# Attention and gated FFN in one kernel: the high parts of the gate and value weights cast on VectorE, and the filler products of the identity tied one behind each stage of a unit

## The chip, the cores and the metric

The kernel runs on one core of one Trainium2 chip. The metric is device time in microseconds (us). Three runs of the kernel before took 1180.95, 1181.29 and 1181.86 us, so the median is 1181.29 us.

A core has these engines: PE (TensorE, matrix products; PEld are its weight loads), DVE (VectorE), ACT (ScalarE), POOL (GpSimd) and SP (SyncE), which here only issues DMAs. Each engine works through its own queue in order. An instruction that needs another engine's result waits on a semaphore, and everything behind it in its queue waits too.

## The reference, cut to what matters

```python
# q_l, k_l, v_l: 8 batches, 8 heads, 512 tokens, 64 dims;  q_g, k_g, v_g: 32 global tokens
# w_gate, w_val: 512 x 1536 float64;  w_out: 1536 x 512 float64
s_l  = concat([q_l @ k_g.T, where(|i - j| <= 32, q_l @ k_l.T, -1e9)]) / 8
out_l = softmax(s_l) @ concat([v_g, v_l])              # local tokens
out_g = softmax(q_g @ concat([k_g, k_l]).T / 8) @ concat([v_g, v_l])
x    = concat([out_g, out_l]) -> (8 * 544 tokens, 8 heads * 64)
y    = (sigmoid(x @ w_gate) * (x @ w_val)) @ w_out
```

The result is needed close to float32. The FFN multiplies with a one-pass format (F32R), so each of its operands is split into a high part and a low part, and three products (high by high, low by high, high by low) are summed. The three weights arrive as float64 and are turned to float32 on the chip.

## The kernel before, in words

The tokens are cut into chunks: chunk 0 is blocks 0 and 1 (of 128 tokens each) of batch 0, chunk 1 is blocks 2 and 3 of batch 0 and its global tokens, and chunks 2 to 8 are batches 1 to 7. Chunk 9 is the FFN of all global tokens. For each chunk the attention of 8 heads is computed and then its FFN in 12 steps f of 128 hidden columns (`ffn_stream`, L384).

**Attention of a unit** (`local_unit`, L224) is two blocks of one head, in four stages: scores on PE (L234); mask and row minimum on DVE (L248) and the exponential on ACT (L251); the sums' reciprocals and the scaling into `p_buf` on DVE (L254, L255, L218); four transposes on PE (L270), copied out by ACT (L278); the products with the values on PE (L293, L294), copied out by ACT (L297). A pair of heads is then split into high and low by ACT and POOL (`x_split`, L370 to L373). Chunk 0 has eight units, one for each head, and nothing to overlap with but each other, since the first FFN product (L400) needs its attention.

**Weights** (`convert`, L128) come in 36 pieces of 128x512, three for each f (gate, value, out). Each one is loaded by SP into one of three buffers (L126), ACT takes the exponent's offset out of the upper words (L137), DVE shifts the lower words and joins the two (L139, L140) into one of two buffers, ACT casts the joined words to F32R, which is the high part (L141), and POOL subtracts it from the joined words, which leaves the low part (L142). Gate and value pieces stay in SBUF (`wg`, `wv`); out pieces go to DRAM and are read back at each FFN step.

**Fillers** (`fill`, L108) are products of the 128x128 identity with itself into a PSUM bank that nobody reads. `FILL = (8, 1)`: eight at the beginning, and one behind each PE stage of a unit of chunk 0 (`T["first"]`; L236, L272, L296), 32 in all. Each appears as two PE records (this holds for every product in plain float32; a transpose is one record).

**What sets the order.** The kernel writes its instructions down in an order that a list of events with due times gives: chunk 0's attention is all due before the FFN stream begins, the conversion of f is due at -2 + 4 f FFN units, and attention of the following chunks lies between FFN steps. The program that is run comes from a scheduler that puts the instructions of each engine in a queue order by when it thinks that they can start, and among those that can, takes what was written first. A filler has no input but the identity, so nothing ties it to the place where it was written. `tc.issue_after(ins)` ties what a block issues behind `ins` on the same engine's queue; it adds no semaphore.

Of the kernel before, what the change touches and what calls it, by code (L numbers as in the profile page):

```python
# [17 lines left out]
P = 128  # L18
# [10 lines left out]
VS = (2, 3, 6, 7)  # L29
# [13 lines left out]

HOLE = (8, 1)

FILL = (8, 1)
START = dict(per0=4, base1=1, per1=1.1, base2=23, per2=3, x2=28, lead=8, native_heads=4)
CONVERT = (-2, 4, 1, 3)
CONVERT_EARLY = (-985, -980, -977)
# [10 lines left out]
def kernel(ctx, tc, qk, v, w_gate, w_val, w_out, out_l, out_g):  # L60
    nc = tc.nc
# [15 lines left out]
    ident = const.tile([P, P], F32, name="ident")  # L77
# [27 lines left out]

    fill_ps = ps.tile([P, DM], F32, name="bank_o3")

    def fill(n):  # L108
        for i in range(n):
            nc.tensor.matmul(fill_ps[:, 0:P], ident, ident, start=True, stop=True)  # L110

    fill(FILL[0])
    conv_bufs = []
    anchor, exp_at = [None], [None]

# [6 lines left out]
    def stage(i):  # L122
        if i < len(w_src):
            src = w_src[i]
            st = conv_bufs[0][i % len(conv_bufs[0])].rearrange("p (t n) -> p t n", t=src.shape[1])
            nc.sync.dma_start(st, src)  # L126

    def convert(i, hi, lo):  # L128

        src = w_src[i]  # L130
        t, n = src.shape[1], src.shape[2] // 2
        st, v = (o[i % len(o)].rearrange("p (t n) -> p t n", t=t) for o in conv_bufs)
        words = st.rearrange("p t (n two) -> p t n two", two=2)
        low, high = words[:, :, :, 0], words[:, :, :, 1]
        vf, hf = v.bitcast(F32), high.bitcast(F32)
        with tc.issue_after(exp_at[0].ins) if i < 3 else nullcontext():
            nc.scalar.activation(hf, hf, AF.Prelu, scale=2.0 ** -112, alpha=-2.0 ** 32)  # L137
        with tc.issue_after(anchor[0].ins) if i < 3 else nullcontext():
            nc.vector.tensor_scalar(v, low, 29, None, op0=ALU.logical_shift_right)  # L139
            nc.vector.scalar_tensor_tensor(v, high, 3, v, op0=ALU.logical_shift_left, op1=ALU.bitwise_or)  # L140
        nc.scalar.copy(hi, vf)  # L141
        nc.gpsimd.tensor_tensor(lo, vf, hi.bitcast(F32), op=ALU.subtract)  # L142
        stage(i + len(conv_bufs[0]))

    def convert_w(f, i):
        fs = slice(f * P, (f + 1) * P)
        w = (wg, wv)[i]
        convert(3 * f + i, w[0][:, :, fs], w[1][:, :, fs])

    def convert_wo(f):  # L150
        hi, lo = (spl.tile([P, 1, DM], F32R, name=nm, tag="kl") for nm in ("wo_hi", "wo_lo"))
        convert(3 * f + 2, hi, lo)
        nc.sync.dma_start(wo_dram[f][:, 0], hi[:, 0].bitcast(F32))
        nc.sync.dma_start(wo_dram[f][:, 1], lo[:, 0].bitcast(F32))


    def qcol(j):
        return j * P if j < 2 else Q1 + (j - 2) * P
# [55 lines left out]
    def scaled(kind, out, in_, by):  # L214
        if NORM[kind][cnt["norm"] % len(NORM[kind])] == "s":
            nc.scalar.mul(out, in_, by)
        else:
            nc.vector.tensor_scalar(out, in_, by, None, op0=ALU.mult)  # L218
        cnt["norm"] += 1

    def span(j):
        return (32 if j == 0 else 0), (WIN - 32 if j == 3 else WIN)

    def local_unit(T, blocks, x32s, h, b0):  # L224
        ks, k0s, q0 = T["qk"], T["k0"], T["q0"]
        nat = T["native"]
        last = len(ks) - 1
        s_ps = ps.tile([P, 2, 256], F32, name="bank_x", tag="att", bufs=4)
        for i, j in enumerate(blocks):
            qj = ks[0][:, qcol(j) - q0:qcol(j) - q0 + P]  # L230
            w0, w1 = span(j)
            for t, (kt, k0) in enumerate(zip(ks, k0s)):
                js = slice(k0 + j * BLK + w0, k0 + j * BLK + w1)
                nc.tensor.matmul(s_ps[:, i, w0:w1], qj, kt[:, js], start=t == 0, stop=t == last)  # L234
        if T["first"]:
            fill(FILL[1])  # L236
        if T["first"]:
            s_sb = ffn.tile([P, 2, WIN], F32, name="s_first", tag="ob", bufs=2)
        else:
            s_sb = att.tile([P, 2, WIN], F32, name="s_sb", bufs=1)  # L240
        nm = small.tile([P, 2], F32, name="nm")
        sm = small.tile([P, 2], F32, name="sm")
        r = small.tile([P, 2], F32, name="r")
        pb = p_bufs[cnt["p"] % 2 if T["first"] else 0]
        cnt["p"] += 1
        for i, j in enumerate(blocks):
            w = slice(*span(j))
            anchor[0] = nc.vector.tensor_tensor_reduce(  # L248
                out=s_sb[:, i, w], in0=s_ps[:, i, w], in1=mid[:, w], scale=-0.125, scalar=3.0e38,
                op0=ALU.add, op1=ALU.min, accum_out=nm[:, i:i + 1])  # L250
            exp_at[0] = nc.scalar.activation(s_sb[:, i, w], s_sb[:, i, w], AF.Exp, bias=nm[:, i:i + 1], scale=-1.0,  # L251
                                             accum_out=sm[:, i:i + 1])
        yield
        nc.vector.tensor_scalar_add(r, sm, 1e-9)  # L254
        nc.vector.reciprocal(r, r)  # L255
        flat = pb.rearrange("p a c -> p (a c)")
        joint = blocks[0] == 0 and blocks[1] == 3
        for i, j in enumerate(blocks):
            main = s_sb[:, i, 32:224].rearrange("p (a c) -> p a c", c=96)[:, :, 0:64]
            m0, s0 = 256 * i, (0 if joint else 256 * i) + P + (64 if j == 3 else 0)  # L260
            scaled(nat, flat[:, m0:m0 + P].rearrange("p (a c) -> p a c", c=64), main, r[:, i:i + 1])
            n = 2 if j in (0, 3) else 3
            side = s_sb[:, i].rearrange("p (a c) -> p a c", c=32)[:, 3 * (j == 0):7:3][:, 0:n]
            scaled(nat, flat[:, s0:s0 + 32 * n].rearrange("p (a c) -> p a c", c=32), side, r[:, i:i + 1])
        yield
        nt = 3 if joint else 4
        side_at = (1, 1) if joint else (1, 3)
        pt_ps = ps.tile([P, 4, P], F32, name="bank_y", tag="att", bufs=4)[:, 0:nt]
        for t in range(nt):
            nc.tensor.transpose(pt_ps[:, t], flat[:, t * P:(t + 1) * P], ident)  # L270
        if T["first"]:
            fill(FILL[1])  # L272
        if nat:
            if T["first"] and h % 2:
                pt = ffn.tile([P, 4, P], F32, name="pt_first", tag="th", bufs=1)[:, 0:nt]
            else:
                pt = att.tile([P, 4, P], F32, name="pt_nat", tag="pt", bufs=1)[:, 0:nt]
            nc.scalar.copy(pt, pt_ps)  # L278
        else:
            pt = att.tile([P, 2, 4, P], F32R, name="pt", bufs=1)[:, :, 0:nt]  # L280
            nc.scalar.copy(pt[:, 0], pt_ps)
            nc.vector.tensor_tensor(pt[:, 1], pt_ps, pt[:, 0].bitcast(F32), op=ALU.subtract)  # L282
        yield
        vt = T["v"]
        if h // 2 not in x32s:
            x32s[h // 2] = att.tile([P, 512], F32, name="x32")
        prow = 64 * (h % 2)
        b1, step = blocks[0] - b0, blocks[1] - blocks[0]
        dst = x32s[h // 2][prow:prow + 64].rearrange("p (i c) -> p i c", c=P)[:, b1:b1 + step + 1:step]
        if nat:  # L290
            o_ps = ps.tile([64, 2, P], F32, name="bank_x", tag="att", bufs=4)
            for i, j in enumerate(blocks):
                nc.tensor.matmul(o_ps[:, i], vt[:, VM[j], :], pt[:, 2 * i], start=True, stop=False)  # L293
                nc.tensor.matmul(o_ps[:, i], vt[:, VS[j], :], pt[:, side_at[i]], start=False, stop=True)  # L294
            if T["first"]:
                fill(FILL[1])  # L296
            nc.scalar.copy(dst, o_ps)  # L297
            return
        o_ps = ps.tile([P, 2, 2, P], F32, name="bank_x", tag="att", bufs=4)
        for i, j in enumerate(blocks):  # L300
            nc.tensor.matmul(o_ps[:, i], vt[:, VM[j], :], pt[:, :, 2 * i, :], start=True, stop=False)  # L301
            nc.tensor.matmul(o_ps[:, i], vt[:, VS[j], :], pt[:, :, side_at[i], :], start=False, stop=True)  # L302
        t0 = att.tile([64, 2, 2, P], F32, name="t0", tag="t0", bufs=1)
        nc.scalar.copy(t0, o_ps[64:128])  # L304
        nc.vector.tensor_tensor(t0, o_ps[0:64], t0, op=ALU.add)  # L305
        nc.gpsimd.tensor_tensor(dst, t0[:, :, 0], t0[:, :, 1], op=ALU.add)  # L306
# [217 lines left out]
    for ci in range(3, G):  # L524
        at, width = HOLE
# [7 lines left out]
    for f in range(NF):  # L533
        at = a0 + f * step
# [83 lines left out]
```

## Time and profile before

The profiled execution took 1179.81 us; its span, from the first instruction to the last, is 1177.9 us, so 1.9 us lie around the span.

| engine | busy us | share of the span | instructions |
|---|---|---|---|
| PE | 1146.4 | 97% | 6596 |
| PEld | 962.3 | 82% | 6596 |
| DVE | 773.7 | 66% | 2132 |
| ACT | 753.2 | 64% | 1737 |
| POOL | 413.3 | 35% | 408 |

A share is a mean over stages with different limits. The beginning (attention of chunk 0 alone), the stretch in which the weights are converted, and the rest have to be read apart. A busy PE is not always useful: the fillers count as busy.

### The profile page before, as it was taken

How to read it: one execution, taken by the hardware profiler on the slowest of the kernel's cores; microseconds unless marked ns; L12 is line 12 of the kernel's file. 1: busy time of each engine (PE TensorE's matmuls, PEld its weight loads, DVE VectorE, ACT ScalarE, POOL GpSimd, SP SyncE). 2: the span in 40 equal slices, each digit the busy share in tenths (PEclk: the TensorE clock that was granted, in tenths of full speed). 3: DMA queues.
4: the chain of work that ended last, by engine and by line, in shares of the span. 5: the costliest groups of instructions: out<-in, count | busy, mean ns of one | idle time of the engine just before them, and what ended most of it. 6: DMA issues, size and time to landing. Idle time of an engine off the chain costs nothing.

```text
span 1177.9 us, 19115 instructions
## 1 busy us (share of the span) xinstructions
PE 1146.4 (97%) x6596; PEld 962.3 (82%) x6596; DVE 773.7 (66%) x2132; ACT 753.2 (64%) x1737; POOL 413.3 (35%) x408
## 2 busy tenths in 40 slices
PE   8999999999999999999999999999999999999998
PEld 7777788888888888888888888888888888888897
DVE  5677657577676677667676677667676677533343
ACT  5898877566675676666675676666675675532343
POOL 2444435334353444334352444334452443100000
PEclk9999999999999999999999999999999999999999
DMA  8888844333443343343343343343344342122143
GB/s 295 283 288 279 259 134 128 95 116 94 115 116 113 106 115 98 106 140 90 113 115 114 105 116 98 107 149 91 103 116 122 99 118 81 44 100 72 54 151 118
DMA packets 59489, 151.81 MB, mean 129 GB/s; under 512 B 6144, under 2 KB 19456, under 8 KB 59392
## 3 DMA queue, kind: packets, MB, share of 16 engines
q1 hardware_dynamic: 59392, 150.59, 42.2%
q8 instruction: 52, 0.85, 0.3%
q14 instruction: 45, 0.37, 0.1%
HBM read 135.36 MB, written 15.20 MB: 128 GB/s over the span
## 4 chain that ended last, share of the span: by engine, by line
PE 75%; DVE 11%; ACT 8%; issue 3%; DMA 2%; POOL 1%; SPq 0%; ACTq 0%; DVEq 0%; POOLq 0%
PE bank_v L400 20%; PE bank_g L400 19%; PE bank_o L437 19%; PE bank_x L234 4%; DVE p_buf L218 4%; PE bank_y L270 4%; ACT s_sb L251 3%; PE bank_x L301 2%; PE bank_x L302 2%; PE bank_x L318 2%; PE bank_x L361 1%; DVE bank_v L420 1%; DVE bank_v L421 1%; PE bank_o L110 1%; ACT hh L423 1%
## 5 line engine op out<-in xcount | busy, mean ns | idle before, releaser
L400 PE MATMUL bank_v<-xt,wv 128*128 128x512 f32 (+1 forms) x1440 | 328.3, 364 | 14.1 <-DVE pt L282 14.1
L400 PE MATMUL bank_g<-xt,wg 128*128 128x512 f32 (+1 forms) x1440 | 330.4, 364 | 0.1
L437 PE MATMUL bank_o<-wo,hh 128*128 128x512 f32 x1224 | 329.2, 400 | 1.2 <-ACT hh L423 1.2
L400 PEld LDWEIGHTS bank_v<-xt,wv 128*128 128x128 f32 x1440 | 237.1, 189 | 51.0 <-issue 16.0
L400 PEld LDWEIGHTS bank_g<-xt,wg 128*128 128x128 f32 x1440 | 236.8, 189 | 37.4 <-issue 2.5
L437 PEld LDWEIGHTS bank_o<-wo,hh 128*128 128x128 f32 x1224 | 217.2, 189 | 41.8 <-ACT hh L423 3.0
L251 ACT ACTIVATE s_sb<-s_sb,nm 128x192 f32<-128x192 f32 (+1 forms) x240 | 110.4, 462 | 98.2 <-DVE nm L248 97.3
L218 DVE TENSOR_SCALAR p_buf<-s_sb,r 128x128 f32<-128x128 f32 (+2 forms) x443 | 153.5, 383 | 6.6 <-PE bank_y L270 1.7
L306 POOL TENSOR_TENSOR x<-t 64x256 f32<-64x256 f32 x104 | 76.4, 735 | 172.1 <-DVE t L305 146.1
L211 POOL TENSOR_TENSOR vhl<-v_raw,vhl 128x512 fp32r<-128x512 f32 x52 | 67.2, 1293 | 187.4 <-ACT vhl L210 104.1
L198 POOL TENSOR_TENSOR kl<-qk_raw,qk_hi 128x704 fp32r<-128x704 f32 x52 | 88.6, 1703 | 108.3 <-ACT qk_hi L197 107.8
L423 ACT CAST hh<-bank_v 128x512 fp32r<-128x512 f32 (+1 forms) x120 | 62.7, 522 | 96.1 <-DVE bank_v L421 95.2
L408 ACT ACTIVATE th<-bank_g 128x512 f32<-128x512 f32 (+1 forms) x120 | 63.7, 531 | 87.0 <-PE bank_g L400 86.6
L413 DVE TENSOR_SCALAR mn<-bank_g 128x512 f32<-128x512 f32 (+1 forms) x108 | 67.4, 624 | 71.8 <-ACT th L408 71.8
L305 DVE TENSOR_TENSOR t<-bank_x,t 64x512 f32<-64x512 f32 x104 | 70.7, 680 | 62.0 <-ACT t L304 61.1
L420 DVE TENSOR_TENSOR bank_v<-bank_v,mn 128x512 f32<-128x512 f32 (+1 forms) x120 | 73.6, 614 | 53.5 <-PE bank_v L400 48.4
L248 DVE CUSTOM_DVE_ANT_0 s_sb<-bank_x,masks 128x192 f32<-128x192 f32 (+1 forms) x240 | 79.9, 370 | 38.5 <-PE bank_x L234 35.6
L424 DVE TENSOR_TENSOR hh<-bank_v,hh 128x512 fp32r<-128x512 f32 (+1 forms) x120 | 73.0, 608 | 35.1 <-ACT hh L423 33.2
L200 POOL TENSOR_TENSOR qk_hi<-qk_raw,qk_hi 64x256 fp32r<-64x256 f32 x104 | 80.3, 792 | 4.1
L421 DVE SCALAR_TENSOR_TENSOR bank_v<-th,bank_v 128x512 f32<-128x512 f32 (+1 forms) x120 | 73.2, 610 | 1.8
L414 ACT ACTIVATE mn<-mn 128x512 f32<-128x512 f32 (+1 forms) x108 | 62.9, 583 | 12.9 <-DVE mn L413 8.2
L270 PE MATMUL bank_y<-ident,p_buf 128*128 128x128 f32 x440 | 69.7, 274 | 1.3 <-ACT mn L410 0.5
(108 smaller groups left out, 1648.7 us busy)
## 6 DMA issues: line engine op xcount, KB each, us to landing
wo<-wo_dram SPq DMA_DIRECT2D x116, 512.0 KB, 3.4
qk_raw<-in_qk_dram SPq DMA_DIRECT2D x104, 312.0 KB, 4.4
v_raw<-in_v_dram SPq DMA_DIRECT2D x52, 256.0 KB, 2.6
out_dram<-ob SPq DMA_DIRECT2D x34, 256.0 KB, 2.9
xt<-in_w_gate_dram SPq DMA_DIRECT2D x12, 512.0 KB, 5.4
xt<-in_w_val_dram SPq DMA_DIRECT2D x12, 512.0 KB, 5.0
xt<-in_w_out_dram SPq DMA_DIRECT2D x12, 512.0 KB, 5.3
v_nat<-in_v_dram SPq DMA_DIRECT2D x8, 512.0 KB, 7.6
```

The costliest lines, as they stand in the source:

```text
L198: nc.gpsimd.tensor_tensor(kl, t[:, K0:Q1], hi[:, K0:Q1].bitcast(F32), op=ALU.subtract)
L200: nc.gpsimd.tensor_tensor(hi[64:128, r], t[64:128, r], hi[64:128, r].bitcast(F32), op=ALU.subtract)
L218: nc.vector.tensor_scalar(out, in_, by, None, op0=ALU.mult)
L248: anchor[0] = nc.vector.tensor_tensor_reduce(out=s_sb[:, i, w], in0=s_ps[:, i, w], in1=mid[:, w], scale=-0.125, scalar=3.0e38, op0=ALU.add ...
L251: exp_at[0] = nc.scalar.activation(s_sb[:, i, w], s_sb[:, i, w], AF.Exp, bias=nm[:, i:i + 1], scale=-1.0, accum_out=sm[:, i:i + 1])
L270: nc.tensor.transpose(pt_ps[:, t], flat[:, t * P:(t + 1) * P], ident)
L306: nc.gpsimd.tensor_tensor(dst, t0[:, :, 0], t0[:, :, 1], op=ALU.add)
L400: nc.tensor.matmul(acc, w[a][:, t, fs], xt[:, c, t, x0:x0 + ntok], start=n == 0, stop=n == 11)
L420: nc.vector.tensor_tensor(acc, acc, mn, op=ALU.mult)
L421: nc.vector.scalar_tensor_tensor(acc, th, 1.0, acc, op0=ALU.add, op1=ALU.mult)
L423: nc.scalar.copy(hh[:, 0, 0:ntok], acc)
L437: nc.tensor.matmul(o_ps[t], ph[:, a, t * P:(t + 1) * P], pwo[:, c], start=f2 == 0 and i == 0, stop=f2 == NF - 1 and i == 2)
```

## The change

The diff, whole but for its file names:

```diff
-FILL = (8, 1)
+FILL = (6, 7, 1)
...
-    def fill(n):
-        for i in range(n):
-            nc.tensor.matmul(fill_ps[:, 0:P], ident, ident, start=True, stop=True)
-
-    fill(FILL[0])
+    def fill(n, at=None):
+        with tc.issue_after(at.ins) if at is not None else nullcontext():
+            for i in range(n):
+                m = nc.tensor.matmul(fill_ps[:, 0:P], ident, ident, start=True, stop=True)
+        return m
+
+    last_fill = fill(FILL[0])
...
-    def convert(i, hi, lo):
+    def convert(i, hi, lo, on_vector):
...
             nc.vector.scalar_tensor_tensor(v, high, 3, v, op0=ALU.logical_shift_left, op1=ALU.bitwise_or)
-        nc.scalar.copy(hi, vf)
+            if on_vector:
+                nc.vector.tensor_copy(hi, vf)
+        if not on_vector:
+            nc.scalar.copy(hi, vf)
         nc.gpsimd.tensor_tensor(lo, vf, hi.bitcast(F32), op=ALU.subtract)
...
-        convert(3 * f + i, w[0][:, :, fs], w[1][:, :, fs])
+        convert(3 * f + i, w[0][:, :, fs], w[1][:, :, fs], True)
...
-        convert(3 * f + 2, hi, lo)
+        convert(3 * f + 2, hi, lo, False)
...
-                nc.tensor.matmul(s_ps[:, i, w0:w1], qj, kt[:, js], start=t == 0, stop=t == last)
-        if T["first"]:
-            fill(FILL[1])
+                with tc.issue_after(last_fill.ins) if T["first"] and h == 0 else nullcontext():
+                    m = nc.tensor.matmul(s_ps[:, i, w0:w1], qj, kt[:, js], start=t == 0, stop=t == last)
+        if T["first"] and h > 0:
+            fill(FILL[1 if h == 1 else 2], m)
...
-            nc.tensor.transpose(pt_ps[:, t], flat[:, t * P:(t + 1) * P], ident)
+            m = nc.tensor.transpose(pt_ps[:, t], flat[:, t * P:(t + 1) * P], ident)
         if T["first"]:
-            fill(FILL[1])
+            fill(FILL[2], m)
...
-                nc.tensor.matmul(o_ps[:, i], vt[:, VS[j], :], pt[:, side_at[i]], start=False, stop=True)
+                m = nc.tensor.matmul(o_ps[:, i], vt[:, VS[j], :], pt[:, side_at[i]], start=False, stop=True)
             if T["first"]:
-                fill(FILL[1])
+                fill(FILL[2], m)
```

So six fillers come first and the scores of head 0 are tied behind them; seven are tied behind the scores of head 1, one behind the scores of each of heads 2 to 7, one behind the transposes and one behind the value products of each of the eight heads: 35 in all. Of the 36 casts of weight pieces, the 24 of gate and value pieces move from ACT to DVE; the 12 of out pieces stay on ACT.

## Rows read from the trace of the kernel before

**Rows 1.** Busy time of each engine in four stretches of the span (columns: stretch, its length, then busy us and instructions of PE, PEld, DVE, ACT and POOL, TensorE's granted clock, the DMA engines' share, GB/s). Chunk 0's attention, two halves of the conversion of weights, and the rest.

```profile
0.00:36.00 36.00, 30.55 (x192) 24.55 (x192) 22.12 (x94) 22.59 (x62) 9.62 (x19) 1.00 0.86 284
36.00:100.00 64.00, 61.78 (x428) 47.07 (x427) 46.38 (x123) 57.68 (x160) 27.71 (x24) 1.00 0.86 282
100.00:145.00 45.00, 43.45 (x278) 34.90 (x278) 33.88 (x95) 38.56 (x107) 19.39 (x15) 1.00 0.87 283
145.00:1178.00 1033.00, 1010.66 (x5704) 855.79 (x5702) 671.35 (x1821) 634.40 (x1411) 356.63 (x352) 1.00 0.36 107
```

**Rows 2.** The instructions of all engines in order of time, up to the scaling of the first two heads (columns: start, us, engine, line, operation, output and inputs, count, and in brackets the idle time before and what ended it).

```profile
1.20 0.29 POOL masks.py:199 TENSOR_SCALAR_AFFINE_SELECT ident<-ident 128x128 f32<-128x128 f32 x1
...
3.75 1.76 PE L234 MATMUL bank_x<-qk_nat 64*128 64x192 f32 x8 [3.75 <-DMA qk_nat<-in_qk_dram]
...
5.44 4.42 PE L110 MATMUL bank_o<-ident 128*128 128x128 f32 x19
5.66 0.36 DVE L248 CUSTOM_DVE_ANT_0 s_first<-bank_x,masks 128x192 f32<-128x192 f32 x1 [4.01 <-PE bank_x L234]
...
7.51 0.87 DVE L218 TENSOR_SCALAR p_buf<-s_first,r 128x128 f32<-128x128 f32 x4
```

**Rows 3.** PE alone in order of time, the first 36 us: the run of fillers and the first transposes, one head without a filler, the shorter runs of fillers with what follows them (a second run of four records, at 25.32, is left out), and the last two heads up to the first FFN product.

```profile
5.44 6.11 PE L110 MATMUL bank_o<-ident 128*128 128x128 f32 x34
11.39 0.38 PE L270 MATMUL bank_y<-ident,p_buf 128*128 128x128 f32 x2
...
13.16 0.71 PE L110 MATMUL bank_o<-ident 128*128 128x128 f32 x4
13.80 0.43 PE L293 MATMUL bank_x<-pt_nat,v_nat 128*64 128x128 f32 x2
...
14.82 0.65 PE L270 MATMUL bank_y<-ident,p_first 128*128 128x128 f32 x4
15.41 0.97 PE L234 MATMUL bank_x<-qk_nat 64*128 64x192 f32 x4
16.30 0.43 PE L293 MATMUL bank_x<-pt_first,v_nat 128*64 128x128 f32 x2
...
17.32 0.66 PE L270 MATMUL bank_y<-ident,p_buf 128*128 128x128 f32 x4
...
18.81 0.49 PE L110 MATMUL bank_o<-ident 128*128 128x128 f32 x2
19.23 0.43 PE L293 MATMUL bank_x<-pt_nat,v_nat 128*64 128x128 f32 x2
...
21.73 1.16 PE L110 MATMUL bank_o<-ident 128*128 128x128 f32 x8
22.82 0.43 PE L293 MATMUL bank_x<-pt_first,v_nat 128*64 128x128 f32 x2
...
28.46 1.60 PE L110 MATMUL bank_o<-ident 128*128 128x128 f32 x12
30.00 0.43 PE L293 MATMUL bank_x<-pt_first,v_nat 128*64 128x128 f32 x2
...
31.01 0.66 PE L270 MATMUL bank_y<-ident,p_buf 128*128 128x128 f32 x4
32.69 0.43 PE L293 MATMUL bank_x<-pt_nat,v_nat 128*64 128x128 f32 x2 [1.03 <-ACT pt_nat L278]
...
33.71 0.66 PE L270 MATMUL bank_y<-ident,p_first 128*128 128x128 f32 x4
35.04 0.43 PE L293 MATMUL bank_x<-pt_first,v_nat 128*64 128x128 f32 x2 [0.68 <-ACT pt_first L278]
...
36.06 0.61 PE L400 MATMUL bank_g<-xt,wg 128*128 128x256 f32 x3
```

**Rows 4.** What PE waited for between 36 and 145 us (columns: who waits, for whom, us in total, times, the longest).

```profile
PE bank_o L437 <- ACT hh L423: 1.2, 3, 0.6
PE bank_y L320 <- DVE mn L413: 0.6, 1, 0.6
PE bank_x L293 <- ACT pt_nat L278: 0.6, 1, 0.6
PE bank_y L270 <- ACT mn L410: 0.5, 1, 0.5
PE bank_y L270 <- ACT p_buf L216: 0.4, 1, 0.4
PE bank_y L270 <- DVE p_buf L218: 0.4, 1, 0.4
```

**Rows 5.** The instructions of single lines, the conversion's casts on ACT (L141) and its two operations on DVE (L139, L140) (ns: shortest, median, longest; first and last start; forms), and the grouped view of L139 over the whole span (busy us, mean ns, idle before).

```profile
L141 ACT CAST wg<-xt x12: 602/619/620, 20.8 to 135.4; 128x512 fp32r<-128x512 f32 x12
L139 DVE TENSOR_SCALAR xt<-xt x36: 412/424/1494, 17.0 to 137.7; 128x512 uint32<-128x512 uint32 x36
L140 DVE SCALAR_TENSOR_TENSOR xt<-xt x36: 675/693/1807, 19.8 to 139.9; 128x512 uint32<-128x512 uint32 x36
...
L139 DVE TENSOR_SCALAR xt<-xt 128x512 uint32<-128x512 uint32 x36 | 20.2, 563 | 14.4 <-POOL wg L142 4.8 <-POOL wv L142 4.7 <-DMA xt<-in_w_out_dram 2.2
```

**Rows 6.** One subtraction on POOL and the join that DVE began beside it, in order of time.

```profile
26.24 1.27 POOL L142 TENSOR_TENSOR wv<-xt,wv 128x512 fp32r<-128x512 f32 x1
...
26.60 1.46 DVE L140 SCALAR_TENSOR_TENSOR xt<-xt 128x512 uint32<-128x512 uint32 x1 [0.50 <-ACT xt L137]
```

## The prediction, as it was recorded

> **What bounds the kernel now.** I read the stages first [rows 1], since shares of the whole span mix three regimes. From 145 us on PE is busy for 1010.7 of 1033 us; nothing in the diff lies there. From 36 to 145 us (weights converted beside attention and FFN) PE is busy for 61.78 + 43.45 = 105.2 of 109 us, so at most 3.8 us can be won there; ACT is the next, 57.68 + 38.56 = 96.2 us or 88%, DVE 46.38 + 33.88 = 80.3 us or 74%. The waits say who keeps PE idle there [rows 4]: ACT ends 1.2 + 0.6 + 0.5 + 0.4 = 2.7 us of it, DVE 0.6 + 0.4 = 1.0 us. The first 36 us are the attention of chunk 0; PE looks busy for 30.55 us, but the order of time shows what with [rows 3]: 34 filler records stand from 5.44 until the first transposes at 11.39, 30 more are spread over the rest, and only at 36.06 does the first FFN product run. That stage is a chain through PE's queue, and the fillers are in it.
>
> Where it starts is seen one level down [rows 2]: head 0's scores begin at 3.75, the mask at 5.66, and `p_buf` is scaled at 7.51 + 0.87 = 8.38. The transposes could have run then; they stand behind the fillers until 11.39, 3.0 us later. The granted clock reads 1.00 throughout [rows 1], but the fillers show both levels: 19 records start between 5.44 and 9.6, 0.219 us apart [rows 2], the other 15 take the 1.8 us to 11.39, 0.12 apart [rows 3]: the lower level (1.2 GHz) first, the upper (2.4 GHz) from about 9.6 on, with PE busy since 3.75.
>
> **The start of chunk 0.** Six fillers now lead. The identity is ready at 1.20 + 0.29 = 1.49 [rows 2]; PE can start at about 1.6, and 12 records at 0.219 take 2.6 us, to 4.2, with a change of tile 4.3. Head 0's scores are tied behind them, so they begin at 4.3 and not at 3.75, which is when their data land: 0.55 us lost. The mask and exponential chain takes what it took, 8.38 - 3.75 = 4.63, so `p_buf` is ready at 8.9 and the transposes can run at 9.0. The seven tied fillers begin 5.44 - 3.75 = 1.69 behind the scores, at 6.0, and 14 records take 3.1 us at the lower level, 1.7 at the upper: done between 7.8 and 9.3. First transposes at 9.1, against 11.39: **-2.3 us**. Ends: -2.9 (leading fillers wholly ahead of the data: 8.5) and -1.8 (all at the lower level, and a late start).
>
> **The loop over heads.** Between first transposes and first FFN product the old kernel spends 36.06 - 11.39 = 24.7 us. Head 1 shows it free of fillers: transposes 15.41 - 14.82 = 0.59, next scores 16.30 - 15.41 = 0.89, values 17.32 - 16.30 = 1.02, in all 2.50 [rows 3]. One filler costs more than its two records. From the start of a run to the values behind it: 2 records 0.42, 4 records 0.64, 8 records 1.09, 12 records 1.54 [rows 3]: 0.2 and 0.111 a record. The 0.2 comes on top at a change of tile (scores are 64*128, fillers 128*128, values 128*64); transposes are 128*128 as a filler is, so behind or ahead of them I take the records alone, 0.22. So a head of the new loop costs 2.50 + 0.22 (behind transposes) + 0.42 (behind scores) + 0.22 (behind values, with transposes next) = 3.36. Six such heads make 20.2 us. The last two have no scores: transposes, then the copy; from 31.01 to 32.69 and 33.71 to 35.04 ([rows 3], 1.68 and 1.33) I take 1.33 twice, with their filler inside that wait, then 1.02 + 0.22 each: 5.1 us. Sum 25.3 against 24.7: **+0.6 us**. Ends: each at 0.42 where it is not hidden adds 6 * 0.40 + 2 * 0.20 = 2.8 (+3.4); no change of tile in it anywhere takes 6 * 0.20 off (-0.6).
>
> The old kernel had 15 fillers in this stretch, the new one 22, so the tie removes a block of 17 and then spends more on singles. What is late next is the chain on DVE and ACT. A head's scores are done 1.7 us behind the transposes two heads earlier and its own transposes are due 6.7 us behind those, so it has 5.0 us; from scores to scaled, 4.63 - 1.69 = 2.9 us are needed. That leaves 2.1 us for conversion steps in between.
>
> **The casts.** 24 casts leave ACT, 0.617 us each [rows 5]: 14.8 us. Four ran before 36 us, 20 between 36 and 145, where ACT falls from 96.2 to 83.9 us (77%). No row shows a float32 cast from SBUF to SBUF on DVE. Rows on both sides, of as many elements, 128x512: 0.412 at the least for the one-input shift, 0.675 at the least for the two-input join; their longest, 1.494 and 1.807, are what a block costs [rows 5]. I take the one-input row with its mean, 0.563, since the cast has one input; 20 * 0.56 = 11.3 us, and DVE rises from 80.3 to 91.6 us of 109 (84%). The Trainium skill's page "VectorE: DVE Perf Modes", section "The perf-mode tier table", lets a one-input SBUF copy or cast of float32 run at two elements a cycle and a two-tensor operation at one; the shift and the join (0.412 and 0.675) agree, and by it the cast would be the former.
>
> The cast now follows the join on its own engine, so the hop to ACT and ACT's queue go, and the subtraction and the release of the joined buffer come sooner; DVE waited 4.8 + 4.7 = 9.5 us for that release [rows 5]. Behind a cast on DVE stand masks, scalings and the FFN's products (L420 to L424), for which PE waits. No wait is new: the cast's input comes from the instruction ahead of it. I halve ACT's 2.7 us of PE waits (-1.35) and let DVE's 1.0 grow by a third (+0.35): **-1.0 us**. Ends: -3.8 (all idle time of the stretch) and the slower rival's price below. SP's loads wait for L139 and L140, whose place stays; POOL does the same work.
>
> **Sum.** -2.3 + 0.6 - 1.0 = -2.7 us. Against the profiled execution, 1179.81 (span 1177.9 and 1.9 around it), that is 1177.1; it ran 1.5 us under the median of the runs, so against 1181.29 the forecast is 1178.6. From 145 us on I count nothing: its order is written down as before, though the scheduler may move single instructions.
>
> **Rivals.**
> - *Both gains are larger.* Leading fillers hidden (-2.9), singles without a change of tile (-0.6), and most of the idle time between 36 and 145 us gone (-3.0): -6.5, 1174.8. For it: ACT ends most PE waits there. Against: 0.42 for the one single filler that is seen.
> - *Singles dear.* Every filler costs 0.42: +3.4 - 2.3 - 1.0 = +0.1, 1181.4. For it: that one row at 18.81. Against: the runs of transposes after fillers at 11.39 show no extra.
> - *The tie brings nothing.* If the leading fillers start late (the old queue had them behind the scores), they run from 3.75 instead of 1.6: transposes at 11.2, -0.2 + 0.6 - 1.0 = -0.6, 1180.7.
> - *Slower: DVE becomes the bound by its blocks with POOL.* A join begun at 26.60 beside a subtraction that ran from 26.24 to 27.51 took 1.46 and not 0.68 [rows 6], so 0.78 lost. If every cast loses that, 20 * (0.42 + 0.78) = 24 us come on DVE, 104 of 109 (96%), where ACT at 88% already let PE idle. With 40% of the 15.6 us lost passed on to PE: +6.2; with -2.3 + 0.6: +4.5, 1185.8. It decides from about 95% of DVE on. Against: the shift's median, 0.424, says that most are not blocked. The Trainium skill's page "SBUF — State Buffer", section "SBUF: two separate sides", says that VectorE in its two-port mode and GpSimd exclude each other for a whole instruction; it speaks for this rival, and the 1.46 us agrees with it.
>
> **How the numbers follow.** Forecast 0.50 (own range 1176.8 to 1180.5), larger 0.20, singles dear 0.12, tie without effect 0.06, slower 0.12. The range leaves out the outer half of the larger case and nearly all of the slower one: 1174.5 to 1182.5. About 0.2% (2.4 us) is what a measurement can tell from no change: faster is below 1178.9, which takes 0.30 of the forecast and all of the larger case: 0.50. Same: 0.20 of the forecast, 0.11 and 0.06: 0.37. Slower 0.13.
>
> **What would show it.** First transposes near 9.1 and first FFN product near 34.4; the leading fillers from about 1.6, and head 0's scores near 4.3; single fillers spaced 0.22 beside transposes and 0.42 behind scores; the DVE cast near 0.56 in the mean; ACT about 84 us and DVE about 92 us busy in a stretch of 109 us, PE's idle time there near 2.8 us. It is wrong if the first FFN product stays at 36 us, if PE's waits on DVE grow past 2 us, or if the stage behind 145 us changes by more than a microsecond.

## The result, and the profile after

The changed kernel takes 1189.21 us (median of 4 runs, 1187.02 to 1191.59); the kernel before took 1181.12 in the same set. The ratio is 1.007, 95% interval 1.0048 to 1.0092: 8.1 us slower, where 2.7 us faster were forecast. The profiled execution has 1187.02 us, span 1184.9.

The stages of the kernel after (columns as in [rows 1]; the last stretch ends with the span):

```profile
0.00:36.00 36.00, 31.09 (x188) 24.45 (x188) 24.40 (x99) 21.28 (x59) 11.31 (x19) 1.00 0.86 300
36.00:100.00 64.00, 58.78 (x375) 45.97 (x375) 48.26 (x129) 50.66 (x142) 27.20 (x22) 0.95 0.81 268
100.00:145.00 45.00, 43.39 (x299) 35.00 (x297) 38.23 (x97) 31.30 (x88) 18.61 (x15) 1.00 0.79 256
145.00:1184.00 1039.00, 1017.22 (x5745) 860.70 (x5743) 673.85 (x1833) 639.87 (x1426) 358.60 (x354) 1.00 0.36 108
```

The damage is in the second row: PE is busy for 58.78 us in place of 61.78, and the granted clock there is 0.95, so part of that busy time is done at half speed. ACT is relieved (50.66 + 31.30 = 82.0 us of 109, 96.2 before) and DVE rises less than forecast (48.26 + 38.23 = 86.5 us, 79%). Neither is a bound.

Where the time comes in is seen by matching the FFN's gate products by their number in both traces. The table gives each kernel's start of a product less that of the kernel before; its first row is where that product starts before. The rows e1 to e11 are the experiments below. Each row is one execution, and that of e6 is its fastest of twelve (1176.78 us, median 1179.82), so its -3.0 is better than it is as a rule.

| us against before | 1st | 13th | 25th | 61st | 151st | last |
|---|---|---|---|---|---|---|
| start before | 36.1 | 42.9 | 54.8 | 98.8 | 152.3 | 1169.0 |
| after | +1.7 | +3.5 | +3.9 | +7.5 | +7.2 | +7.0 |
| e1 fillers alone | 0.0 | +1.8 | +6.5 | +7.3 | +7.9 | +8.9 |
| e2 casts alone | +3.8 | +5.8 | +7.5 | +9.2 | +9.3 | +8.5 |
| e3 | +1.4 | +1.5 | +1.5 | +5.0 | +4.8 | +5.1 |
| e4 | +1.3 | +2.4 | +2.4 | +4.0 | +3.8 | +3.3 |
| e5 casts, old order | -0.5 | +2.0 | +6.8 | +11.7 | +17.8 | +17.6 |
| e6 fillers, old order | -1.2 | -1.5 | -1.5 | -1.5 | -2.3 | -3.0 |
| e7 both, old order | -1.1 | +0.8 | +3.9 | +8.8 | +13.4 | +14.8 |
| e10 casts late | -1.4 | -0.1 | +0.1 | +0.5 | -0.4 | +0.5 |
| e11 both, casts late | -1.7 | -0.8 | -0.7 | -0.2 | +2.2 | +1.6 |

All is lost before the 61st product, in three places: 1.7 us up to the first product, 1.8 at about 42, and 3.6 between 55 and 99. Behind 145 us nothing is added.

The start went as planned. All engines of the kernel after in order of time (columns as in [rows 2]):

```profile
1.54 2.93 PE L111 MATMUL bank_o<-ident 128*128 128x128 f32 x12 [1.54 <-POOL ident masks.py:199]
...
4.40 1.76 PE L240 MATMUL bank_x<-qk_nat 64*128 64x192 f32 x8
...
6.10 1.94 PE L111 MATMUL bank_o<-ident 128*128 128x128 f32 x14
...
8.51 0.33 PE L276 MATMUL bank_y<-ident,p_buf 128*128 128x128 f32 x1 [0.46 <-DVE p_buf L223]
```

The transposes start at 8.51 in place of 11.39, and the loop over heads has the period that was worked out: 12.32, 15.73, 19.14. At that period it would come to the first transposes of the last two heads at 29.4 (25.96 + 3.41), 1.6 us ahead of the kernel before (31.01 in [rows 3]). Its end is another matter. PE alone, the last two heads (answers to the end of [rows 3]):

```profile
30.12 0.33 PE L276 MATMUL bank_y<-ident,p_buf 128*128 128x128 f32 x1 [0.50 <-DVE p_buf L223]
31.32 0.74 PE L276 MATMUL bank_y<-ident,p_buf 128*128 128x128 f32 x3 [0.87 <-DVE p_buf L223]
...
32.74 0.43 PE L299 MATMUL bank_x<-pt_nat,v_nat 128*64 128x128 f32 x2 [0.45 <-ACT pt_nat L284]
...
36.49 0.43 PE L299 MATMUL bank_x<-pt_first,v_nat 128*64 128x128 f32 x2 [1.55 <-ACT pt_first L284]
...
37.76 0.61 PE L406 MATMUL bank_g<-xt,wg 128*128 128x256 f32 x3
```

Four waits, 3.4 us together where the kernel before has 1.7 [rows 3], stand there, and the first FFN product starts 1.7 us late. The last wait has a history on three engines: the copy `pt_first` stands on ACT behind the cast of `wo_hi` (35.34), which waits 1.05 us for a join on DVE (34.58), which stands behind the cast `wv` (34.25).

PE's waits of 36 to 145 us after (answers to [rows 4]):

```profile
PE bank_o L443 <- ACT hh L429: 2.1, 2, 1.3
PE bank_g L406 <- POOL xt L379: 1.6, 1, 1.6
PE bank_x L299 <- ACT pt_first L284: 1.6, 1, 1.6
PE bank_y L276 <- DVE mn L419: 1.4, 1, 1.4
```

Before, no wait there was longer than 0.6 us; now four are 1.3 to 1.6. And a wait has an echo. Windows of the kernel after around two of them:

```profile
40.00:42.00 2.00, 0.40 (x4) 0.20 (x2) 2.00 (x7) 1.01 (x4) 2.00 (x3) 1.00 1.05 402
42.00:46.00 4.00, 3.97 (x21) 3.17 (x22) 1.72 (x6) 2.88 (x9) 1.48 (x1) 0.74 1.06 383
46.00:50.00 4.00, 4.00 (x25) 3.43 (x24) 3.13 (x10) 3.00 (x9) 1.28 (x1) 0.83 0.51 187
...
94.00:98.00 4.00, 2.91 (x13) 2.68 (x14) 2.71 (x7) 3.28 (x8) 0.46 (x1) 0.64 0.63 221
98.00:102.00 4.00, 2.89 (x14) 1.87 (x12) 2.64 (x8) 1.95 (x6) 1.61 (x2) 0.93 0.14 27
```

PE is idle from 40.40 to 42.03 and from 93.70 to 95.09; behind each its clock is below 1. Half speed accounts for (0.26 + 0.17 + 0.36 + 0.07) * 4 = 3.4 us at most, nearly half of what is lost. Not every wait has this echo: behind those of 1.55 us at 36.49 and of 1.30 at 70.38 the clock stayed at 1.00.

The second of these places shows what the change does to DVE's queue. DVE, POOL and PE in order of time:

```profile
90.80 1.30 POOL L147 TENSOR_TENSOR wo_lo<-xt,wo_hi 128x512 fp32r<-128x512 f32 x1 [1.33 <-ACT wo_hi L146]
91.05 1.59 DVE L142 SCALAR_TENSOR_TENSOR xt<-xt 128x512 uint32<-128x512 uint32 x1
...
92.68 0.43 DVE L144 CAST wg<-xt 128x512 fp32r<-128x512 f32 x1
...
93.19 1.27 POOL L147 TENSOR_TENSOR wg<-xt,wg 128x512 fp32r<-128x512 f32 x1 [1.09 <-DVE r L260]
...
93.42 1.29 DVE L223 TENSOR_SCALAR p_buf<-s_sb,r 128x128 f32<-128x128 f32 x2
...
95.09 0.47 PE L276 MATMUL bank_y<-ident,p_buf 128*128 128x128 f32 x1 [1.39 <-DVE mn L419]
```

The join is held up by one subtraction, the cast follows it, and half a microsecond later the cast's own subtraction holds up the scalings; `mn` stands behind them, and with it the wait of the transposes ends. A scaling beside a subtraction is not new by itself (the kernel before has one at 41.06, shown further down); that PE waits 1.39 us here is. Of the four long waits of PE this is the only one that was followed back to a DVE command held up by a cast's own subtraction. The cast itself is cheap. Its single instructions:

```profile
L144 DVE CAST wg<-xt x12: 399/423/551, 17.8 to 137.5; 128x512 fp32r<-128x512 f32 x12
L144 DVE CAST wv<-xt x12: 405/416/916, 23.8 to 140.5; 128x512 fp32r<-128x512 f32 x12
```

### The profile page after: what moved, and what is told of

It reads as the page before. It is cut to its first block, busy times and chain, and to the rows that moved or that the text cites. A ratio compares the mean times of both kernels' runs of the same rounds, so it can differ in the third digit from the quotient of the medians.

```text
span 1184.9 us, 19127 instructions
## 1 busy us (share of the span) xinstructions
PE 1150.5 (97%) x6602; PEld 966.1 (82%) x6602; DVE 784.7 (66%) x2156; ACT 743.1 (63%) x1713; POOL 415.7 (35%) x408
## 4 chain that ended last, share of the span: by engine, by line
PE 75%; DVE 12%; ACT 6%; DMA 3%; issue 2%; POOL 1%; SPq 0%; ACTq 0%; DVEq 0%; POOLq 0%
PE bank_v L406 20%; PE bank_g L406 20%; PE bank_o L443 19%; DVE p_buf L223 4%; PE bank_x L240 3%; PE bank_y L276 3%; ACT s_sb L257 3%; PE bank_x L324 2%; PE bank_x L307 2%; PE bank_x L308 2%; PE bank_x L367 1%; DMA xt<-in_w_out_dram 1%; DVE bank_v L426 1%; DVE bank_v L427 1%; DVE mn L419 1%
```

## The experiments

**Half the change each.** e1 has the fillers of the change and leaves the casts on ACT; e2 has the casts and leaves the fillers.

```diff
e1 (from after)
-        convert(3 * f + i, w[0][:, :, fs], w[1][:, :, fs], True)
+        convert(3 * f + i, w[0][:, :, fs], w[1][:, :, fs], False)
e2 (from before)
+            if on_vector:
+                nc.vector.tensor_copy(hi, vf)
...
+        convert(3 * f + i, w[0][:, :, fs], w[1][:, :, fs], True)
```

> The fillers as in the changed kernel, all 36 casts on ScalarE as before. If the casts on VectorE make the changed kernel slow (theory A), this one has the first transposes near 8.5 us, the first FFN product near 34 to 35 us, and is 1 to 3 us faster than before (1178 to 1180). If the tied fillers and the order that they bring do it (theory B), the first FFN product stays at 37 us or later and the time is 1185 to 1189.

> The 24 casts on VectorE, the fillers untied as before. Theory A: slower than before by most of what the changed kernel lost plus what its fillers won, 1184 to 1190, with VectorE late for the last heads' scalings and waits of PE above 1 us between 36 and 110 us. Theory B: within 2 us of before, 1179 to 1183.

Measured: e1 1190.73 us, ratio 1.0067 (1.0039 to 1.0095); e2 1188.77, 1.004 (1.0011 to 1.0068). Each half alone loses about what both lose together. So neither "the casts are to blame" nor "the fillers are to blame" can be read from these two. e1 has its first FFN product at 36.06, between the places that theories A and B gave it, and its time is above both ranges; e2 is in theory A's range. What both have in common is an order of the queues that the scheduler made anew. In e1, PE waits 2.73 us from 41.85 for a scaling on ACT; the exponentials ahead of it stand behind a step of the conversion (L139, at 40.75) that waited 1.84 us for a load. The windows behind that wait show the longest echo:

```profile
46.00:50.00 4.00, 4.00 (x17) 3.05 (x16) 3.33 (x9) 2.54 (x8) 2.22 (x2) 0.54 0.87 331
50.00:54.00 4.00, 4.00 (x16) 2.70 (x16) 0.60 (x4) 2.90 (x10) 0.00 (x0) 0.50 0.08 24
54.00:58.00 4.00, 4.00 (x21) 3.51 (x21) 0.93 (x3) 1.42 (x4) 0.35 (x1) 0.68 0.95 330
```

From 46 to 58 us PE is busy all the time and goes at 50 to 68% of its pace: (0.46 + 0.50 + 0.32) * 4 = 5.1 us.

**One wait removed, and one filled.** e3 is the changed kernel with one ordering edge on POOL: the subtraction of the third gate piece stands behind the low part of x, for which PE waited from 40.40. In the kernel after it stands ahead (POOL in order of time):

```profile
39.45 1.66 POOL L147 TENSOR_TENSOR wg<-xt,wg 128x512 fp32r<-128x512 f32 x1 [1.83 <-DVE wg L144]
41.08 0.90 POOL L379 TENSOR_TENSOR xt<-x,xt 128x256 fp32r<-128x256 f32 x1
```

e4 leaves the wait and puts six products of the identity into it.

```diff
e3 (from after)
+        with tc.issue_after(low_at[0].ins) if i == 6 else nullcontext():
+            nc.gpsimd.tensor_tensor(lo, vf, hi.bitcast(F32), op=ALU.subtract)
e4 (from after)
+                            if n_it == 0 and nm == "bank_g" and n == 11:
+                                fill(6, m)
```

> The changed kernel with one order on GpSimd put back: the subtraction of the gate piece of f = 2 is tied behind the low part of x of heads 6 and 7 of chunk 0, as it stood in the kernel before. If that order makes PE wait 1.6 us at 42 us and the fall of the clock behind it is a consequence, the wait goes, the clock stays up there, and the time falls by about 3.3 us (1.6 of wait, 1.7 of clock) against the changed kernel. If the clock falls for another reason, only 1.6 us or less are won.

> The changed kernel with six more products of the identity in the 1.6 us in which PE waits at 40 to 42 us, 1.3 us of work. If PE's idle time brings the clock down to half between 42 and 46 us, the clock stays at the upper level and about 1.7 us are won though work is added. If the fall does not come from the idle time, the time is that of the changed kernel or up to 1 us more.

Measured: e3 1186.71 us, ratio 1.0033 (1.0009 to 1.0057); e4 1183.62, 1.0017 (0.9995 to 1.0039). In e3 the step at 42 us is gone from the table, the one before 99 stays with its clock (0.91 in 80 to 100 us); 2.5 us come back by the medians, of the 3.3 expected. e4 adds work and is 5.6 us faster than the changed kernel, where 1.7 were expected; its granted clock is 1.00 in all windows. Some of that is again a slightly different order, so e4 alone doesn't size the clock's part; e12 does.

**The order held.** From here on every engine's queue, DMA queues included, has the order of the kernel before, written down as a table and bound with ordering edges. e5 moves only the casts, each directly behind its join; e6 moves only the fillers; e7 does both.

```diff
e5 (from before, order held)
+            j = nc.vector.scalar_tensor_tensor(v, high, 3, v, op0=ALU.logical_shift_left, op1=ALU.bitwise_or)
+        if on_vector:
...
+            pin.extra.append((nc.vector.tensor_copy(hi, vf).ins, j.ins))
+        else:
+            nc.scalar.copy(hi, vf)
...
+            for a, b in zip(line, line[1:]):
+                tc.add_manual_dep(b, a.name, mybir.DependencyInfo(
+                    mybir.DependencyClass.NoSync, mybir.DependencyReason.DATA), reason="pinned order")
```

> The order of every engine's queue and of every DMA queue is held to that of the kernel before; only the 24 casts go from ACT to DVE, each right behind its join, and the products of the identity stay as they were. Theory C (the new order that the scheduler gives the queues is what loses the time, not the casts): 1178 to 1182 us, no stretch of 36 to 145 us under a granted clock of 0.95, and the first FFN product within 1 us of 36.06. Rival A (the casts themselves cost, since every DVE command behind them is later by 0.4 to 0.9 us): 1184 to 1189 us, with a wait of PE for DVE of over 1 us in that stretch and a lower clock behind it.

> The order of every queue is held to that of the kernel before; only the products of the identity move to their new places (six first, seven behind head 1's scores, one behind each stage), and all casts stay on ACT. Theory C: the first transposes come near 8.5 us instead of 11.39, the first FFN product near 34.5 to 36 us, and the time is 1177 to 1181 us. Rival B (an early start of the loop over heads runs into the loads and conversions whatever the order, so that PE waits behind 30 us and its clock falls): 1184 to 1190 us, with PE waits of 1.5 us or more between 30 and 50 us.

> Both parts of the change with the order of every queue held to that of the kernel before. Theory C: about the sum of the two single runs' differences, 1176 to 1181 us, so 8 to 13 us below the changed kernel, with a granted clock of 1.00 in all stages behind 12 us. Rivals A and B: 1184 to 1190 us, as the changed kernel.

Measured: e5 1196.08 us, ratio 1.0132 (1.0116 to 1.0147); e6 1179.82, 0.9999 (0.9984 to 1.0013); e7 1194.57, 1.0129 (1.0114 to 1.0144). For the fillers theory C holds: by the medians the same fillers lose 9.4 us in e1 (7.9 by the ratio) and nothing in e6. The early start even arrives. From PE of e6 in order of time, the first FFN product:

```profile
34.87 0.60 PE L447 MATMUL bank_g<-xt,wg 128*128 128x256 f32 x3
```

34.87 in place of 36.06; but the median is only 0.4 us below that of before, within the interval. For the casts theory C falls: in the old order they cost 15.9 us, twice what the changed kernel loses, so the scheduler had mended part of it. Rival A has the direction (a long wait of PE, a lower clock behind it), but e5 and e7 lie above its range of 1184 to 1190 us. What they do is best seen at 41 us, where e5's PE waits 2.21 us. First the kernel before, DVE, ACT and POOL in order of time:

```profile
38.97 1.24 DVE L140 SCALAR_TENSOR_TENSOR xt<-xt 128x512 uint32<-128x512 uint32 x1
...
40.25 0.62 ACT L141 CAST wg<-xt 128x512 fp32r<-128x512 f32 x1 [0.16 <-DVE xt L140]
40.47 0.15 DVE L254 TENSOR_SCALAR r<-sm 128x2 f32<-128x2 f32 x1
...
40.94 1.28 POOL L142 TENSOR_TENSOR wg<-xt,wg 128x512 fp32r<-128x512 f32 x1 [1.28 <-ACT wg L141]
41.06 1.24 DVE L218 TENSOR_SCALAR p_buf<-s_sb,r 128x128 f32<-128x128 f32 x1
```

Then e5, the same place:

```profile
39.40 1.24 DVE L184 SCALAR_TENSOR_TENSOR xt<-xt 128x512 uint32<-128x512 uint32 x1
...
40.68 0.43 DVE L187 CAST wg<-xt 128x512 fp32r<-128x512 f32 x1
...
41.19 1.38 POOL L190 TENSOR_TENSOR wg<-xt,wg 128x512 fp32r<-128x512 f32 x1 [1.09 <-DVE wg L187]
41.36 1.23 DVE L302 TENSOR_SCALAR r<-sm 128x2 f32<-128x2 f32 x1
...
43.15 0.42 ACT L462 ACTIVATE mn<-mn 128x256 f32<-128x256 f32 x1 [2.18 <-DVE mn L461]
...
43.91 0.33 PE L318 MATMUL bank_y<-ident,p_buf 128*128 128x128 f32 x1 [2.21 <-ACT p_buf L264]
```

The addition `r`, 128x2 elements, takes 1.23 us: it starts 0.17 us behind the subtraction (41.19) and ends with it (42.59 against 42.57). Before, it was through (40.62) when the subtraction began. Two things turned the two around. Counted from the start of the join, the subtraction begins 0.18 us sooner (1.79 against 1.97), and the addition 0.46 later (1.96 against 1.50), since the cast's 0.43 us now stand ahead of it. The reciprocal, `mn`, the scalings on both engines and the transposes are in line behind it. Before, the subtraction held up a scaling instead (41.06, 1.24 us), while ACT did the other three of the four, and PE waited 0.4 us [rows 4]: what a hold-up costs depends on what stands behind the command that it meets. Over 24 to 145 us the grouped rows of that line, first of the kernel before:

```profile
L254 DVE TENSOR_SCALAR r<-sm 128x2 f32<-128x2 f32 x16 | 3.1, 195 | 1.9 <-ACT s_sb L251 1.8
```

and of e5:

```profile
L302 DVE TENSOR_SCALAR r<-sm 128x2 f32<-128x2 f32 x14 | 10.1, 719 | 1.4 <-ACT s_sb L299 1.4
```

The mean goes from 195 to 719 ns: seven of the 14 take 1.14 us or more in e5, and none over 0.47 in the kernel before. In the changed kernel, with the scheduler's order, the mean is 283 ns and one addition takes 0.96 us, so there the additions are a small part of the loss.

**Which casts, and another place for them.** e8 moves the gate casts alone, e9 the value casts alone, e10 all of them but each behind the next run of scalings in DVE's queue (or ahead of the next join), e11 the same with the new fillers.

```diff
e8 (from e5); in e9 the last argument is i == 1
-        convert(3 * f + i, w[0][:, :, fs], w[1][:, :, fs], True)
+        convert(3 * f + i, w[0][:, :, fs], w[1][:, :, fs], i == 0)
e10 (from e5), e11 (from e7)
+                    while line[at].name not in self.joins | self.scalings:
+                        at += 1
+                    while line[at].name in self.scalings:
+                        at += 1
+                    line.insert(at, x)
```

> As the casts alone in the order of the kernel before, but only the eight gate casts go to DVE (four are left per kind of weight in the first 60 us); the value casts stay on ACT. Theory D (each cast directly behind its join lets the subtraction on POOL start at once, and that holds up the short command that is next on DVE, the reciprocal's addition or a scaling, by about a microsecond): the loss goes with the number of casts that stand ahead of such a command, so about half of the 15.9 us, 1186 to 1190 us. Rival (one place alone loses it, the one behind the gate piece near 41 us, and its clock fall): 1191 to 1196 us here and near 1181 us with the value casts alone.

> The same with only the value casts on DVE and the gate casts on ACT. Theory D: 1186 to 1190 us. Rival (one place): near 1181 us, if the gate piece near 41 us is the place, else 1191 us or more here.

> All gate and value casts on DVE, the order of the kernel before, but each cast stands behind the next run of scalings in DVE's queue (or ahead of the next join, where that comes first) in place of directly behind its join. The same work on the same engines. Theory D: the additions behind the joins take 0.15 us again in place of 1.2, the waits of PE at 41 to 44 us go, and the time is 1178 to 1184 us. Rival E (DVE simply has too much work, or the raw pieces that come free later hold up the loads): 1190 us or more.

> The same late casts together with the new places of the products of the identity. Theory D: the run before it less up to 1 us, 1177 to 1184 us; if it comes under 1178 us it beats the kernel before. Rival E: 1190 us or more.

(The first of these texts counts the casts wrongly: there are twelve of each kind.) Measured: e8 1192.15 us, ratio 1.0092 (1.0065 to 1.0120); e9 1185.20, 1.0039 (1.0022 to 1.0056); e10 1181.10, 1.0005 (0.9988 to 1.0022); e11 1180.12, 0.9999 (0.9985 to 1.0013). The loss doesn't go by the number of casts, as theory D had it: the gate casts cost 12.2 us and the value casts 5.3. e8 has the 2.2-us wait at 41 us and a clock of 0.72 in 36 to 60 us, e9 has neither. So the places are unequal; by the trace e8 loses 8.2 of its 13.8 us between the first and the 25th product, where the wait at 41 us and its clock lie. On the mechanism D is borne out in the main: e10 has the work of e5 on the same engines, and 15 us less. Its place at 41 us:

```profile
40.41 0.15 DVE L312 TENSOR_SCALAR r<-sm 128x2 f32<-128x2 f32 x1
...
41.01 0.28 DVE L276 TENSOR_SCALAR p_buf<-s_sb,r 128x128 f32<-128x128 f32 x1
...
41.20 0.42 DVE L197 CAST wg<-xt 128x512 fp32r<-128x512 f32 x1
41.70 1.27 POOL L200 TENSOR_TENSOR wg<-xt,wg 128x512 fp32r<-128x512 f32 x1 [2.09 <-DVE wg L197]
41.88 0.83 PE L328 MATMUL bank_y<-ident,p_buf 128*128 128x128 f32 x4 [0.62 <-ACT p_buf L274]
42.04 0.43 DVE L479 SCALAR_TENSOR_TENSOR bank_v<-th,bank_v 128x256 f32<-128x256 f32 x1
```

Addition and scaling are done before the subtraction begins, and what runs beside it, `bank_v` in PSUM, takes 0.43 us as ever. PE waits 0.62 us. But the additions do not all come back to 0.15 us, as was expected. Over 24 to 145 us in e10:

```profile
L312 DVE TENSOR_SCALAR r<-sm 128x2 f32<-128x2 f32 x16 | 5.9, 369 | 1.6 <-ACT s_sb L309 1.6
```

Two still take 1.24 us (at 46.8 and 59.0). At 46.8 the cast stands between two joins, close behind its own as in e5, and PE has other products to run meanwhile; its longest wait from 36 to 150 us is 0.9 us. So that hold-up cost PE nothing. And e10 takes two things out of the way of the short commands at once, the subtraction and the cast's own time; no run separates them. At 41 us the trace of e5 sizes them: 1.08 us of hold-up (1.23 less 0.15) and 0.43 us of cast.

Rival E, too much work on DVE or raw pieces that come free late, falls: DVE has 84.9 us of 109 here, more than e5's 82.1. e11 is the whole change with another order, 9.1 us below the changed kernel by the medians, and even with the kernel before. It doesn't beat it.

**What the clock costs.** e12 is e5 with products of the identity in its two longest waits.

```diff
e12 (from e5)
+        fills = [nc.tensor.matmul(pt_ps[:, 0], ident, ident, start=True, stop=True).ins
+                 for _ in range(8 if pin.nu == 8 else 0)]
...
+            fills = [nc.tensor.matmul(o, ident, ident, start=True, stop=True).ins
+                     for _ in range(6 if pin.ng == 0 and j == 0 else 0)]
```

> The casts directly behind their joins in the order of the kernel before (the slowest order so far, 1196.08 us), with products of the identity put into the two longest waits of PE alone: eight ahead of the transposes that waited 2.21 us at 41.7, six ahead of those that waited 1.77 us at 73.8. They write the bank that the transposes then overwrite; nothing else is moved and no wait is shortened. If a part of the loss is the granted clock that falls behind a wait, the windows of 36 to 80 us stay at a clock near 1.00 in place of 0.79 and 0.92, and (1 - 0.79) x 24 + (1 - 0.92) x 20 = 6.6 us come back: 1188 to 1191 us. If the waits alone cost the time, or the clock falls for another reason: 1195 us or more.

Measured: 1192.77 us, ratio 1.0091 (1.0070 to 1.0112), so 3.3 us below e5 by the medians (4.8 by the ratios) and not 6.6; the time lies between the two ranges. The windows of e5:

```profile
36.00:60.00 24.00, 21.18 (x104) 15.88 (x102) 16.16 (x40) 14.28 (x42) 8.13 (x6) 0.79 0.65 217
60.00:80.00 20.00, 17.32 (x108) 12.99 (x107) 13.79 (x40) 14.71 (x41) 7.04 (x6) 0.92 0.79 258
```

and of e12:

```profile
36.00:60.00 24.00, 21.94 (x140) 17.01 (x141) 18.02 (x47) 17.50 (x51) 10.04 (x8) 1.00 0.80 260
60.00:80.00 20.00, 18.75 (x145) 14.71 (x143) 15.38 (x39) 13.90 (x40) 7.96 (x6) 1.00 0.79 254
```

The clock stays at 1.00, as expected of the first case. Up to the 25th product e12 is 3.9 us ahead of e5 by the trace (+2.9 against +6.8). Behind 80 us other waits are longer than in e5 (2.54 us from 112.96, 1.42 there), and the clock of 140 to 160 us is 0.83 against 0.88. So the clock's share was sized up to twice too large; that PE waits again for part of what it wins by speed fits the later waits, and is not shown by a run of its own.

## Why the prediction was wrong

- *The start of chunk 0, -2.3.* Right, and a little better: leading fillers at 1.54 (1.6), scores at 4.40 (4.3), first transpose at 8.51 (9.1), the other three at 9.28.
- *The loop over heads, +0.6.* The period is 3.41 us (3.36). The singles behind scores take 0.42, as priced; those beside transposes some 0.32 (12.75 to 13.07), not 0.22, so not all of the extra comes with a change of tile. That the period fits is partly luck: four transposes with a filler behind them take 0.43 (12.32 to 12.75) where 0.59 were priced. And in e6, with the old order, the loop and the last two heads take 26.6 us (8.25 to 34.87), 1.9 more than the 24.7 of the kernel before and not 0.6.
- *The last two heads.* Here the first term was lost. "I take 1.33 twice, with their filler inside that wait" supposed that scalings and copies come as before; PE waited 0.50 + 0.87 us for the scaling of one head, 0.45 and 1.55 for the copies of both, with conversions in another order around them. The first FFN product stood at 37.76, not 34.4. With the old order (e6) it comes at 34.87: the early start can be carried through, and whether it arrives is decided by the queues of DVE, ACT and POOL. That it then saves time is not shown: e6's median can't be told from that of the kernel before.
- *The casts, -1.0.* This is the step that failed. Their size was overrated if anything (0.42 us in the median and 0.44 in the mean, 0.56 taken; ACT 82.0 and DVE 86.5 us, 83.9 and 91.6 forecast). But the prediction counted it as a gain that the subtraction would "come sooner" and wrote "No wait is new". In its place the changed kernel has four waits of 1.3 to 1.6 us where none was over 0.6, and PE's waits on DVE grow from 1.0 to 2.4 us, which the prediction itself had named as a sign of being wrong. What it overlooked is best seen in e5: the cast pushes the short command behind it back by its own time, the subtraction comes a little sooner, and the subtraction then holds that command up, though a chain to PE hangs on it. The same casts cost 15.9 us directly behind the joins (e5) and 1.2 us by the medians behind the scalings (e10, which can't be told from nothing).
- *The slower rival* had the right pair of engines and about half the price (+4.5 to 1185.8; 8.1 measured), but the wrong condition: "It decides from about 95% of DVE on". DVE is at 79% in the changed kernel and at 75% in e5. In e10 DVE is at 78%, and nothing is lost. So not DVE's sum decides, but which command stands behind the cast. What spoke against it, a shift's median of 0.424, was the wrong row: 9.5 of the 14.4 us idle before the shifts end with a subtraction [rows 5], so most shifts start behind it and say little of a command that starts beside it. The additions and the scalings are the commands to ask about.
- *The order.* "the scheduler may move single instructions" was said of the stretch behind 145 us, and there nothing was lost. Ahead of it a new order was put at nothing without a reason, and that failed too: e1 against e6 shows 11 us between two orders with the same fillers (8 by the ratios).
- *The clock* was in no rival. Behind 36 us no wait of the kernel before is longer than 0.6 us [rows 4], and its clock reads 1.00; in the changed kernel the falls came behind the waits of 1.63 and 1.39 us.

The Trainium skill, page "SBUF — State Buffer", section "SBUF: two separate sides", says that a VectorE instruction in a two-port mode, or with two inputs in SBUF, and a GpSimd instruction shut each other out: whichever starts first keeps the shared ports for its whole instruction. The 1.23 us of a 0.15-us addition in e5, which ends with the subtraction, agrees; so do the 0.43 us of the operations in e10 with an operand in PSUM, which that rule leaves free.

How the changed kernel's own 8 us divide among its three places and the clock is not settled to the microsecond: e3 and e4 each moved other instructions too. That an order of the queues, with the places of the casts in it, makes up the whole of it is shown by e11, which has the same work and loses nothing.

## What to carry to other kernels

Moving an operation to another engine moves the moment at which its consumer starts. Where that consumer holds up commands of the new engine, ask which of them are next in the queue: put the operation behind the short commands that PE waits for, not directly behind its producer. And before the parts of a change are priced one by one, hold the order of all queues and measure them so; with a free scheduler each part alone may look as bad as the whole.

## What was not expected of the hardware

- A command of 128x2 elements took 1.23 us beside a POOL subtraction (0.15 alone), as long as the subtraction lasted; commands with an operand in PSUM took their usual 0.43 us beside one, and a reciprocal of 128x2 its usual 0.17 (93.22 in the changed kernel).
- Several waits of PE of 1.39 to 2.73 us were followed by stretches at a granted clock of 0.50 to 0.83 (down to the level of 1.2 GHz) while PE was already busy again. They are dearer than they look: 5.1 us of pace behind e1's wait of 2.73 us. Others were not: the clock stayed at 1.00 behind a wait of 1.55 us in the changed kernel and behind one of 2.54 us in e12 (112.96 to 115.50), which had nothing put into it. In e12 the wait at 41 us was cut to 1.44 us of idle time and then products of the identity, and the clock behind it stayed at 1.00, where that of e5 fell to 0.50.
